# First scores in four banks, idle matmuls ahead of the loads, and other places for loads and conversions: an attention and mixing kernel on one core

## The chip, the core and the metric

The kernel runs on one core of a Trainium2 chip. The metric is the device time of one execution in microseconds; the median of three runs before the change is 418.61 us. The engines named are TensorE (PE; its weight loads stand as PEld), VectorE (DVE), ScalarE (ACT), GpSimd (POOL) and SyncE (SP), which here only issues loads and stores. ScalarE issues some of the first loads too.

## What is computed

Three blocks follow one another: local attention with a few global keys, a mixing block with a phase, and a gated feed-forward block. Cut to what matters:

```python
# attention: B=2, H=8, S=768, D=64; n_global=8, n_local=96
scores = scale * q @ k.T + bias(head, distance)       # masked to the local band and the global keys
a = exp(scores - max); a = a / (sum(a) + 1e-9)
x = a @ v                                             # heads side by side: [B, 768, 512]
# mixing
theta = x @ w_theta
y = w_tok_r @ (x * cos(theta)) + w_tok_i @ (x * sin(theta))   # along the tokens
u = x + y
x2 = u + relu(u @ w_ch)
# feed-forward
h = relu(x2 @ w_in)
c = depthwise_conv3(h, conv_w)
out = (h * sigmoid(c)) @ w_out
```

The weights w_theta, w_tok, w_ch, w_in, conv_w and w_out come as 64-bit floats.

## The kernel before

**Start.** `begin` (L942) loads the two words n_global and n_local and, for heads 0 and 1, q and k: three loads on SyncE's queue and three on ScalarE's (L950 to L953). A pair of heads shares one tile `qk`: the k of both stands in its two partition halves, the q of each beside zeros (`pad_q`), so that a score matmul runs over all 128 partitions. VectorE works out from the two words a flag `fi`, which says whether the fast path fits, and the mask table `Dt`. `build` then loads the flag on every engine and branches (L933, L936). `run_fast` (L799) is the fast path; the general path is not run here.

**Attention.** A step j is two query tiles of 128 rows of one head; there are 3 steps to a head and 48 steps (`NJ`). A step's parts are staggered over the loop of L834: at turn j TensorE makes the scores of step j into a bank S (two banks in turn), VectorE the softmax of step j-1 (L321, it reads the bank and writes `sS`, three buffers in turn), ScalarE the exponentials of j-2 (L330), TensorE the transposes of j-3 (L339), ScalarE their copy of j-4, TensorE the product with v of j-5 into a bank O (two in turn, one for a head), and VectorE the normalisation of a head (L274 to L276). In turns 0 to 7 VectorE also scales a mask table per head (L292). A head needs its v (`load_v`, L258, three buffers) and every second head the q and k of the next pair (`load_qk`, L224 and L225, two tiles). `load_qk_second` (L230) brings head 1's q. Each engine works through its own list in the order in which the code records it; nothing is reordered. SyncE's list of loads is one queue of this kind, too: a load that waits for a buffer holds all loads behind it.

**Theta and the conversions beside the attention.** After every sixth step the heads of 128 columns are transposed (`transpose_x`, L437, into a bank X), copied to `xT`, and split into two parts for two-part products (`split_xT`). From about step 34 on, theta of batch 0 is worked out, six matmuls a step, in the bank TH. A weight passes through six pieces: load, a (ScalarE, L117), b (VectorE, L122 and L123), c (VectorE, L129 and L130), d (ScalarE's rounding, L101) and e (VectorE's remainder, L109). `Net.weight` puts them on a list, and `net.run(k)` at the end of a turn records the next k of them. Four weights of w_theta and the first eight of w_tok, 72 pieces, are worked off in the attention's loop; the load of weight k+1 is recorded with the piece load of weight k. The number of pieces per turn is set by the last line of the loop:

```python
net.run(1 if j == 3 else 0 if j < 9 else 2)
```

**End of the attention.** When the last head is normalised, the last 128 columns are transposed in two halves, each into the only bank X (L860 to L863), with VectorE copying in between. Four theta products of batch 1 are opened meanwhile (`theta1_open`). Then `tail` follows (L620): the token products, w_ch, the feed-forward block.

Of the kernel before, what the change touches and what calls it, by code (L numbers as in the profile page):

```python
# [12 lines left out]
F32 = mybir.dt.float32  # L13
# [3 lines left out]
ALU = mybir.AluOpType  # L17
AX = mybir.AxisListType

B, H, S, D = 2, 8, 768, 64  # L20
DM, DFF = H * D, 1024
P = 128
NT = S // P
KC = DM // P
NF = DFF // P
NH = B * H
NG = 8
NPREV = P - NG
# [192 lines left out]
def load_qk(nc, io, t, i):  # L221


    nc.sync.dma_start(t[0:D, S:QK], io["qk"][i // 2, 0])  # L224
    nc.sync.dma_start(t[D:P, 0 : S + KK], io["qk"][i // 2, 1])  # L225


def load_qk_second(nc, io, t):

    nc.sync.dma_start(t[D:P, 0:S], io["qk"][0, 1][:, 0:S])  # L230


def pad_q(nc, t):
    nc.gpsimd.memset(t[D:P, S + KK : QK], 0.0)
    nc.gpsimd.memset(t[0:D, 0:S], 0.0)
# [45 lines left out]
class FastAttention(Attention):  # L281
# [15 lines left out]
    def scores(self, j):  # L297
        i, tp = divmod(j, 3)
        net = self.net
        Q, K = self.Q(i), self.K(i)  # L300
        sp = net.bank("S", 2)
        for u in range(2):
            t = 2 * tp + u
            if t == 0:
                o, r = sp[:, P : 2 * P], K[:, 0:P]
            else:
                o, r = sp[:, 256 * u : 256 * u + 256], K[:, KW * (t - 1) + NG : KW * t + P]
            net.mm(o, Q[:, t * P : t * P + P], r, True, True)
        self.state[j] = {"sp": sp}
# [98 lines left out]
class Mix:  # L408
# [6 lines left out]
    def begin(self):  # L415
        n = self.net
        self.xT = [n.slot(f"xT{b}", [P, KC, S], F32, "xT") for b in range(2)]
        wth = n.slot("w", [P, 2, KC, DM], F32R, "wth")
        self.wth = [wth[:, i] for i in range(2)]
        self.r = n.slot("r", [P, NT, DM], F32, "r")  # L420
        n.plan()
        for c in range(KC):
            n.weight(DM, self.wth[0][:, c], self.wth[1][:, c])
        self.wt = [[n.slot("p0", [P, 4, 2, HALF], F32R, "wt"), n.slot("p1", [P, 4, 2, HALF], F32R, "wt"), None], [None] * 3]
# [2 lines left out]
        n = self.net  # L427
        self.xTs = [n.slot(f"y{i}", [P, KC, S], F32R, "xTs") for i in range(2)]

    def transpose_x(self, b, c, e="A"):  # L430

        n = self.net
        for hf in range(2):
            xb = n.bank("X")
            for jj in range(3):
                t = 3 * hf + jj
                self.nc.tensor.transpose(xb[:, P * jj : P * jj + P], self.xs[b][:, t, P * c : P * c + P], n.head["ident"])  # L437
            yield
            n.hi(e, self.xT[b][:, c, HALF * hf : HALF * hf + HALF], xb[:, 0:HALF])
# [359 lines left out]
def run_fast(tc, net):  # L799
    nc, io = net.nc, net.io  # L800
    xs = [net.slot(f"xs{b}", [P, NT, DM], F32, "xs") for b in range(2)]
    att = FastAttention(net, xs)
    mix = Mix(net, xs)
    att.load_v(0)
    load_qk_second(nc, io, att.qk[0])
    att.load_v(1)
    load_qk(nc, io, att.qk[1], 2)
    mix.begin()
    mix.load_tok(0, 0)
    mix.load_tok(0, 1)  # L810
    net.drain()
    mix.alloc_xTs()
    NJ = 3 * NH
    OPEN = [NJ + 4, NJ + 6, NJ + 7, NJ + 8]
    first, last, splits, theta0 = Pipe(), Pipe(), deque(), None

    def theta_0():
        for t in range(NT):
            tiles = mix.theta(t, "TH", 1)
            for k in range(2):  # L820
                for _ in range(6):
                    th = next(tiles)
                yield
            first.add(mix.reduce_theta(th, mix.r[:, t]))

    early = mix.trig0()

    def split(b, c):
        yield
        yield  # L830
        yield
        splits.append((b, c))

    for j in range(NJ + LAG_N + 3):  # L834
        i, tp = divmod(j, 3)
        if j < NJ:
            att.scores(j)
        first.step()
        if 0 <= j - LAG_SM < NJ:
            att.softmax(j - LAG_SM)  # L840
        if tp == 0 and i < H:
            att.table(i)
        if 0 <= j - LAG_EXP < NJ:
            att.exps(j - LAG_EXP)
        if 0 <= j - LAG_T < NJ:
            att.transposes(j - LAG_T)
        if 0 <= j - LAG_EV < NJ:
            att.evacuate(j - LAG_EV)
        if 0 <= j - LAG_PV < NJ:
            att.pv(j - LAG_PV)  # L850
        jj = j - LAG_N
        if 0 <= jj < NJ and jj % 3 == 2:
            att.normalise(jj // 3, att.o.pop(jj // 3))
        if tp == 2 and i % 2 and i + 3 < NH:
            load_qk(nc, io, att.qk[i // 2 % 2], i + 3)
        if 0 < i < NH - 1 and tp == 2:
            att.load_v(i + 1)
        last.step()
        jj = j - LAG_N - 1
        if jj == NJ - 1:  # L860
            for chain in (mix.transpose_x(1, KC - 1, "V"), mix.split_xT(1, KC - 1, "V")):
                for _ in chain:
                    pass  # L863
        elif 0 <= jj < NJ and jj % 6 == 5:
            bc = divmod(jj // 6, KC)
            last.add(mix.transpose_x(*bc), split(*bc))
        if splits and (splits[0][0] == 0 or theta0 == "done"):
            b, c = splits.popleft()
            last.add(mix.split_xT(b, c, "V"))
            if (b, c) == (0, KC - 1):  # L870
                theta0 = theta_0()
        elif theta0 and theta0 != "done" and next(theta0, last) is last:
            theta0 = "done"
            mix.alloc_xTs()
        if j in OPEN:
            mix.theta1_open(OPEN.index(j))
        if j >= NJ + 4:
            next(early, None)
        net.run(1 if j == 3 else 0 if j < 9 else 2)
    last.drain()  # L880
    mix.tail(early)

# [37 lines left out]
def arm(tc, io, head, run):  # L920
    with tc.tile_pool(name="small", bufs=1) as small, tc.tile_pool(name="slots", bufs=1) as slots, tc.tile_pool(
        name="ps", bufs=1, space=bass.MemoryType.PSUM
    ) as ps, tc.manual_schedule():
        run(tc, Net(tc, io, small, slots, ps, head))


def build(nc, io):
    with tile.TileContext(nc) as tc, tc.tile_pool(name="const", bufs=1) as small:
        head = {}
        net = Net(tc, io, small, None, None, head)  # L930
        with tc.manual_schedule():
            begin(nc, io, net, small, head)
        rv = nc.values_load(  # L933
            head["flag"][:1, :1], min_val=0, max_val=1, skip_runtime_bounds_check_because="it is the product of comparisons, 0 or 1"
        )
        with tc.If(rv == 1) as cmp:  # L936
            arm(tc, io, head, run_fast)
        with cmp.Else():
            arm(tc, io, head, run_general)


def begin(nc, io, net, small, head):  # L942

    w = small.tile([P, 4], I32, name="words")
    scratch = small.tile([P, 2560], F32, name="scratch")
    nc.sync.dma_start(w, io["n"].bitcast(I32).rearrange("(o n) -> o n", o=1).to_broadcast([P, 4]))
    qk0 = small.tile([P, QK], F32, name="qk0")
    two, one = io["qk"][0, 0], io["qk"][0, 1]
    ks, qs = (slice(0, 2 * KW), slice(2 * KW, KK)), (slice(KK, KK + 2 * P), slice(KK + 2 * P, KK + S))
    for e, k, q in ((nc.sync, ks[0], qs[0]), (nc.scalar, ks[1], qs[1])):  # L950
        e.dma_start(qk0[0:D, S + k.start : S + k.stop], two[:, k])
        e.dma_start(qk0[D:P, S + k.start : S + k.stop], one[:, S + k.start : S + k.stop])
        e.dma_start(qk0[0:D, S + q.start : S + q.stop], two[:, q])  # L953
    pad_q(nc, qk0)
    cwb = small.tile([P, 2 * NF * 3], I32, name="cwb")

# [18 lines left out]
    ng, nl = f[:, 6:7], f[:, 7:8]  # L975
    flag = small.tile([1, 2], F32, name="flag")
    fi = small.tile([1, 1], I32, name="fi")
    nnl = small.tile([P, 1], F32, name="nnl")
    nc.vector.tensor_scalar(flag[:, 0:1], nl[0:1], 1.0, None, op0=ALU.is_ge)
    nc.vector.tensor_scalar(Dt[:, 0 : 2 * P], R[:, 0 : 2 * P], nl, BIG, op0=ALU.is_ge, op1=ALU.mult)  # L980
    nc.vector.scalar_tensor_tensor(flag[:, 1:2], nl[0:1], float(NPREV + 1), flag[:, 0:1], op0=ALU.is_le, op1=ALU.mult)
    nc.vector.tensor_scalar(Dt[:, NPREV:P], R[:, NPREV:P], ng, BIG, op0=ALU.is_ge, op1=ALU.mult)
    nc.vector.scalar_tensor_tensor(fi, ng[0:1], float(NG), flag[:, 1:2], op0=ALU.is_le, op1=ALU.mult)
    nc.vector.tensor_tensor(Dt[:, 0:NPREV], Dt[:, 0:NPREV], R[:, 0:NPREV], op=ALU.max)
    nc.vector.tensor_tensor(Dt[:, P : 2 * P], Dt[:, P : 2 * P], R[:, P : 2 * P], op=ALU.max)
    nc.vector.tensor_scalar(Dt[:, NPREV:P], Dt[:, NPREV:P], nl, None, op0=ALU.max)
# [39 lines left out]
```

## Time and profile before

| what | value |
|---|---|
| median of three runs | 418.61 us (418.59 to 419.8) |
| the profiled execution: its time | 418.75 us |
| its span, first instruction to last | 416.5 us |
| TensorE busy | 403.7 us, 97% |
| VectorE busy | 318.4 us, 76% |
| ScalarE busy | 236.8 us, 57% |
| first score matmul starts | 6.12 us |

The span is what the trace shows; 2.2 us of the execution's time lie around it. All times in the trace count from the span's start. A busy engine is one with an instruction under way. A matmul's end is modelled and overlaps with the next one's start, so that the distance from start to start tells more than a duration. A wait is put down to the semaphore that came last. In the row of granted clocks, as in the busy rows, a 9 is nine tenths or more. A product of 32-bit floats shows as two matmuls in the trace and as one in the order of instructions.

### The profile page before, as it was taken

Reading aid. Unit: us, or ns where it says so; the run is one execution under the profiler, and the core shown is the slowest. Engines: PE = TensorE matmul, PEld = TensorE weight load, DVE = VectorE, ACT = ScalarE, POOL = GpSimd, SP = SyncE. Lnnn points to the kernel's source line nnn. Section 1 sums busy time; section 2 is a strip of 40 time slices with the busy share of each in tenths; the row PEclk is TensorE's granted clock in tenths of the full one; section 3 lists DMA queues with packets and bytes.
Section 4 is the critical chain, followed back from the end, with each engine's and each line's share of the span. In section 5 each row is a group of like instructions: output and inputs, shape, how many; then the busy total and the mean of one; then the engine's idle time right before and its main releaser. Section 6 shows DMA issues by size and latency. Waiting matters only on the chain.

```text
span 416.5 us, 6402 instructions
## 1 busy us (share of the span) xinstructions
PE 403.7 (97%) x2376; PEld 379.2 (91%) x2376; DVE 318.4 (76%) x733; ACT 236.8 (57%) x449; POOL 4.4 (1%) x14
## 2 busy tenths in 40 slices
PE   4899999999999999999999999999999999999995
PEld 3899999988897899999999999999999998888885
DVE  4579999667568997899999999999699999800001
ACT  2777888685669536864436245446776889300000
POOL 4000000000000000000000000000000000000000
PEclk9999999999999999999999999999999999999999
DMA  6965776441420004006564352221000000111111
GB/s 168 255 177 178 214 226 161 123 131 35 142 84 2 0 9 144 2 1 188 178 202 155 101 169 84 63 91 52 0 2 0 2 0 0 53 49 50 52 50 58
DMA packets 13095, 38.03 MB, mean 91 GB/s; under 512 B 1856, under 2 KB 2304, under 8 KB 13056
## 3 DMA queue, kind: packets, MB, share of 16 engines
q1 hardware_dynamic: 12816, 37.13, 29.3%
q10 hardware_dynamic: 240, 0.41, 0.4%
q8 instruction: 20, 0.33, 0.3%
q14 instruction: 19, 0.16, 0.1%
HBM read 34.39 MB, written 3.15 MB: 90 GB/s over the span
## 4 chain that ended last, share of the span: by engine, by line
PE 95%; DMA 3%; DVE 1%; SPq 0%; issue 0%; DVEq 0%
PE O L112 26%; PE S L112 26%; PE PT L112 16%; PE TH L112 13%; PE X L112 9%; PE PT L339 4%; DMA qk<-qk 2%; PE X L437 1%; DMA words<-n 1%; SPq L258 0%; DVE a L321 0%; DVE xT L105 0%; SPq L224 0%; SPq L230 0%; DVE scratch L105 0%
## 5 line engine op out<-in xcount | busy, mean ns | idle before, releaser
L112 PE MATMUL S<-qk 128*128 128x256 f32 (+1 forms) x192 | 48.7, 380 | 7.4 <-DMA qk<-qk 7.2
L330 ACT ACTIVATE a<-a,nm 128x256 f32<-128x256 f32 (+1 forms) x96 | 41.5, 482 | 10.4 <-DVE nm L321 10.4
L321 DVE CUSTOM_DVE_ANT_0 a<-S,a 128x256 f32<-128x256 f32 (+1 forms) x96 | 34.5, 399 | 14.4 <-PE PT L339 12.3
L112 PEld LDWEIGHTS S<-qk 128*128 128x128 f32 x192 | 32.6, 198 | 11.1 <-issue 7.6
L101 ACT ACTIVATE a<-PT 128x512 f32<-128x512 f32 (+1 forms) x48 | 26.6, 554 | 11.2 <-PE PT L339 10.8
L112 PE MATMUL O<-a,a 128*128 128x65 f32 x236 | 29.8, 268 | 0.0
L112 PEld LDWEIGHTS O<-a,a 128*128 128x128 f32 x236 | 28.8, 192 | 0.0
L112 PE MATMUL PT<-wt,z 128*128 128x384 f32 x144 | 28.1, 335 | 0.0
L339 PE MATMUL PT<-ident,a 128*128 128x128 f32 x176 | 27.1, 273 | 0.0
L112 PE MATMUL O<-wt,z 128*128 128x384 f32 x144 | 26.9, 334 | 0.0
L339 PEld LDWEIGHTS PT<-ident,a 128*128 128x128 f32 x176 | 22.2, 141 | 4.5
L112 PE MATMUL S<-wt,z 128*128 128x384 f32 x144 | 26.2, 335 | 0.0
L101 ACT ACTIVATE wt<-wbit 128x384 fp32r<-128x384 f32 x24 | 12.5, 521 | 23.9 <-DVE wbit L130 23.9
L112 PE MATMUL TH<-wth,xTs 128*128 128x512 f32 x96 | 25.9, 406 | 0.0
L112 PEld LDWEIGHTS PT<-wt,z 128*128 128x128 f32 x144 | 25.3, 188 | 0.0
L112 PEld LDWEIGHTS O<-wt,z 128*128 128x128 f32 x144 | 25.2, 188 | 0.1
L112 PEld LDWEIGHTS S<-wt,z 128*128 128x128 f32 x144 | 25.2, 188 | 0.0
L117 ACT ACTIVATE wbit<-wst 128x384 f32<-128x384 f32 (+1 forms) x33 | 20.2, 612 | 3.3 <-DVE wout L109 1.1
L130 DVE SCALAR_TENSOR_TENSOR wbit<-wst,wbit 128x384 int32<-128x384 int32 (+1 forms) x33 | 20.6, 623 | 1.1
L129 DVE SCALAR_TENSOR_TENSOR wbit<-wst,wbit 128x384 int32<-128x384 int32 (+1 forms) x33 | 20.5, 622 | 0.9
L123 DVE TENSOR_SCALAR wbit<-wbit 128x512 int32<-128x512 int32 (+1 forms) x48 | 18.9, 394 | 1.6
L112 PEld LDWEIGHTS TH<-wth,xTs 128*128 128x128 f32 x96 | 17.1, 189 | 3.2
(180 smaller groups left out, 872.6 us busy)
## 6 DMA issues: line engine op xcount, KB each, us to landing
wst<-w_tok SPq DMA_DIRECT2D x17, 384.0 KB, 4.6
a<-v SPq DMA_DIRECT2D x16, 357.5 KB, 4.8
qk<-qk SPq DMA_DIRECT2D x14, 396.0 KB, 5.7
out<-scratch SPq DMA_DIRECT2D x11, 256.0 KB, 2.0
qk<-w_tok SPq DMA_DIRECT2D x7, 384.0 KB, 3.3
wst<-w_out SPq DMA_DIRECT2D x5, 512.0 KB, 3.4
wst<-w_theta SPq DMA_DIRECT2D x4, 512.0 KB, 7.6
qk<-w_in SPq DMA_DIRECT2D x4, 512.0 KB, 3.4
```

Of the source, the lines that this page charges most:

```text
L101: self.nc.scalar.activation(out, in_, AF.Copy)
L112: self.nc.tensor.matmul(out, l, r, start=start, stop=stop)
L117: self.nc.scalar.activation(t.bitcast(F32), w[:, 1 : w.shape[1] : 2].bitcast(F32), AF.Abs)
L123: nc.vector.tensor_scalar(t, t, 3, 0x3FFFFFFF, op0=ALU.logical_shift_left, op1=ALU.bitwise_and)
L129: nc.vector.scalar_tensor_tensor(t, lo, 29, t, op0=ALU.logical_shift_right, op1=ALU.bitwise_or)
L130: nc.vector.scalar_tensor_tensor(t, hi, -(1 << 30), t, op0=ALU.bitwise_and, op1=ALU.bitwise_or)
L321: nc.vector.tensor_tensor_reduce(sS[:, c], s["sp"][:, c], self.T[i % H][:, 256:TW] if t0 else self.T[i % H][:, 0:256], scale=-0.125, scala ...
L330: self.nc.scalar.activation(sS[:, rng[u]], sS[:, rng[u]], AF.Exp, bias=nm[:, u : u + 1], scale=-1.0)
L339: self.nc.tensor.transpose(pt[:, c], sS[:, c], net.head["ident"])
L437: self.nc.tensor.transpose(xb[:, P * jj : P * jj + P], self.xs[b][:, t, P * c : P * c + P], n.head["ident"])
```

## The change

It has five parts.

1. `warm` sets 128 columns of scratch to zero on VectorE and puts eleven 128x128 products of them on TensorE, ahead of the flag's load, into a bank of a pool that ends with `begin`.
2. The first loads of q and k: both parts of q go on ScalarE's queue and ahead of its k; SyncE's queue carries the words and its part of k. The flag is computed ahead of the mask table.
3. Steps 0 to 3 have their scores recorded in turns 0 and 1, into the banks S, S, X and TH; turns 2 and 3 record none.
4. The load of q and k of heads 2 and 3 is recorded ahead of v of head 1. The numbers of pieces per turn become 1 in turn 5, 1 and 2 in turns 10 to 31, 2 and 3 from turn 32 on.
5. The second half of the last transposes goes into a bank O.

The diff, cut (the banks' argument is also passed through `transpose_x`, and the two flag instructions move up by two lines):

```diff
-        sp = net.bank("S", 2)
+        sp = net.bank("X") if j == 2 else net.bank("TH") if j == 3 else net.bank("S", 2)
...
-            xb = n.bank("X")
+            xb = n.bank(*second) if hf else n.bank("X")
...
     load_qk_second(nc, io, att.qk[0])
+    load_qk(nc, io, att.qk[1], 2)
     att.load_v(1)
-    load_qk(nc, io, att.qk[1], 2)
...
-        if j < NJ:
-            att.scores(j)
+        for x in ((0, 1), (2, 3), (), ())[j] if j < 4 else (j,) if j < NJ else ():
+            att.scores(x)
...
-            for chain in (mix.transpose_x(1, KC - 1, "V"), mix.split_xT(1, KC - 1, "V")):
+            for chain in (mix.transpose_x(1, KC - 1, "V", ("O", 2)), mix.split_xT(1, KC - 1, "V")):
...
-        net.run(1 if j == 3 else 0 if j < 9 else 2)
+        net.run(1 if j == 5 else 0 if j < 10 else 1 + j % 2 if j < 32 else 2 + j % 2)
...
+def warm(nc, z, idle):
+    nc.vector.memset(z, 0.0)
+    o = idle.tile([P, 512], F32, name="idle")
+    for _ in range(11):
+        nc.tensor.matmul(o[:, 0:P], z, z, start=True, stop=True)
...
+    warm(nc, scratch[:, 2432:2560], idle)
...
-    for e, k, q in ((nc.sync, ks[0], qs[0]), (nc.scalar, ks[1], qs[1])):
+    for x, (k, q) in enumerate(zip(ks, qs)):
+        nc.scalar.dma_start(qk0[0:D, S + q.start : S + q.stop], two[:, q])
+        e = nc.scalar if x else nc.sync
         e.dma_start(qk0[0:D, S + k.start : S + k.stop], two[:, k])
         e.dma_start(qk0[D:P, S + k.start : S + k.stop], one[:, S + k.start : S + k.stop])
-        e.dma_start(qk0[0:D, S + q.start : S + q.stop], two[:, q])
```

SyncE's queue right behind the branch, before the change. The tiles a_3, a_4 and a_5 hold v, qk_63 the tile of heads 0 and 1, qk_6 that of heads 2 and 3, wst the raw weights:

```order
L936 COMPARE_AND_BRANCH
L258 DMA a_3_130<-v 128x715
L230 DMA qk_63<-qk 64x768
L258 DMA a_4_131<-v 128x715
L224 DMA qk_6_133<-qk 64x1584
L225 DMA qk_6_133<-qk 64x1584
L144 DMA wst_145<-w_theta 128x1024
L144 DMA wst_146<-w_theta 128x1024
L224 DMA qk_63<-qk 64x1584
```

The same place after the change (qk_79 is the tile of heads 0 and 1):

```order
L936 COMPARE_AND_BRANCH
L258 DMA a_3_147<-v 128x715
L230 DMA qk_79<-qk 64x768
L224 DMA qk_6_150<-qk 64x1584
L225 DMA qk_6_150<-qk 64x1584
L258 DMA a_4_148<-v 128x715
L224 DMA qk_79<-qk 64x1584
L225 DMA qk_79<-qk 64x1584
L258 DMA a_5_149<-v 128x715
L144 DMA wst_162<-w_theta 128x1024
L144 DMA wst_163<-w_theta 128x1024
```

The second v and the two loads of heads 2 and 3 have changed places, and the first two weights stand behind the loads of heads 4 and 5 and the third v.

TensorE at the start, before the change; S, PT and O are banks, the first product from qk_6 is head 2's:

```order
L933 TENSOR_LOAD fi
L936 COMPARE_AND_BRANCH
L112 MATMUL S_152<-qk_63 128x128
L112 MATMUL S_152<-qk_63 128x256
L112 MATMUL S_156<-qk_63 128x256 x2
L112 MATMUL S_162<-qk_63 128x256 x2
L112 MATMUL S_170<-qk_63 128x128
L112 MATMUL S_170<-qk_63 128x256
L339 MATMUL PT_179<-ident,a_5_132 128x128 x3
L112 MATMUL S_185<-qk_63 128x256 x2
```

The same after the change:

```order
L947 MATMUL idle<-scratch 128x128 x11
L933 TENSOR_LOAD fi
L936 COMPARE_AND_BRANCH
L112 MATMUL S_169<-qk_79 128x128
L112 MATMUL S_169<-qk_79 128x256
L112 MATMUL S_172<-qk_79 128x256 x2
L112 MATMUL X_176<-qk_79 128x256 x2
L112 MATMUL TH_179<-qk_79 128x128
L112 MATMUL TH_179<-qk_79 128x256
L339 MATMUL PT_196<-ident,a_5_149 128x128 x3
L112 MATMUL S_200<-qk_79 128x256 x2
```

TensorE's list is the same but for the idle products and the banks of the third and fourth step.

VectorE around the second weight's pieces b (L122, L123) and c (L129, L130), before the change; the lines L321 are a softmax:

```order
L321 ISA a_5_132,nm_378<-S_350,a_4_131 128x256
L321 ISA nm_378 128x1
L122 TENSOR_SCALAR wbit_318<-wbit_318 128x512
L123 TENSOR_SCALAR wbit_318<-wbit_318 128x512
L129 SCALAR_TENSOR_TENSOR wbit_318<-wst_146,wbit_318 128x512
L130 SCALAR_TENSOR_TENSOR wbit_318<-wst_146,wbit_318 128x512
L321 ISA a_5_132,nm_405<-S_375,a_4_131 128x256
```

After the change, for the same weight:

```order
L122 TENSOR_SCALAR wbit_360<-wbit_360 128x512
L123 TENSOR_SCALAR wbit_360<-wbit_360 128x512
L321 ISA a_5_149,nm_463<-S_437,a_4_148 128x128
L321 ISA nm_463 128x1
L321 ISA a_5_149,nm_463<-S_437,a_4_148 128x256
L321 ISA nm_463 128x1
L109 TENSOR_TENSOR xTs_168<-xT_158,xTs_167 128x768
L129 SCALAR_TENSOR_TENSOR wbit_360<-wst_163,wbit_360 128x512
```

The four passes stood in one row between two softmaxes; now a softmax stands between b and c.

## Rows read from the trace of the kernel before

**Rows 1.** The page: busy tenths and granted clock in 40 slices of 10.4 us

```profile
PE   4899999999999999999999999999999999999995
...
DVE  4579999667568997899999999999699999800001
...
PEclk9999999999999999999999999999999999999999
```

**Rows 2.** Waits of TensorE, whole run: us in total, times, longest us

```profile
PE S L112 <- DMA qk<-qk: 7.2, 2, 6.1
PE X L437 <- DVE xT L105: 0.7, 1, 0.7
```

**Rows 3.** Timeline, 0 to 16 us: start us, us, engine line op, count [idle before <-releaser]

```profile
4.25 0.33 DVE L980 TENSOR_SCALAR Dt<-scratch,nf 128x256 f32<-128x256 f32 x1
...
4.75 0.14 DVE L983 SCALAR_TENSOR_TENSOR fi<-nf,flag 1x1 int32<-1x1 f32 x1
...
5.54 0.35 SPq L258 DMA_DIRECT2D a<-v  x1
...
5.93 0.47 SPq L230 DMA_DIRECT2D qk<-qk  x1
...
7.58 0.59 SPq L225 DMA_DIRECT2D qk<-qk  x1
...
10.33 0.52 PEld L112 LDWEIGHTS S<-qk 128*128 128x128 f32 x4 [0.33 <-issue]
...
14.02 0.78 PE L112 MATMUL O<-a 128*128 128x65 f32 x6
...
15.91 0.89 PE L112 MATMUL S<-qk 128*128 128x128 f32 x4 [1.10 <-DMA qk<-qk]
```

**Rows 4.** Loads L230, v of head 1, L225, first w_theta: KB each, us to landing

```profile
qk<-qk SPq DMA_DIRECT2D x1, 192.0 KB, 3.9
...
a<-v SPq DMA_DIRECT2D x1, 357.5 KB, 5.6
...
qk<-qk SPq DMA_DIRECT2D x1, 396.0 KB, 8.2
...
wst<-w_theta SPq DMA_DIRECT2D x1, 512.0 KB, 8.9
```

**Rows 5.** TensorE by form, 6 to 9.2 and 11.4 to 14 us: xcount | busy, mean ns

```profile
L112 PE MATMUL S<-qk 128*128 128x256 f32 x6 | 2.8, 634 | 0.0
...
L112 PE MATMUL S<-qk 128*128 128x256 f32 x8 | 2.1, 380 | 0.0
```

**Rows 6.** Timeline of VectorE and of TensorE, 52 to 54 us

```profile
52.34 0.56 DVE L130 SCALAR_TENSOR_TENSOR wbit<-wst,wbit 128x384 int32<-128x384 int32 x1
...
52.71 0.78 PE L112 MATMUL O<-a 128*128 128x65 f32 x6
53.64 0.92 PE L112 MATMUL S<-qk 128*128 128x128 f32 x4
```

**Rows 7.** Timeline of TensorE, 129 to 131 us: the last transposes

```profile
129.17 0.49 PE L437 MATMUL X<-ident,xs 128*128 128x128 f32 x3
130.31 0.55 PE L437 MATMUL X<-ident,xs 128*128 128x128 f32 x3 [0.65 <-DVE xT L105]
130.62 0.72 PE L112 MATMUL S<-wth,xTs 128*128 128x512 f32 x2
```

**Rows 8.** Timeline of ScalarE and of TensorE, 22 to 29 us

```profile
22.11 0.68 ACT L117 ACTIVATE wbit<-wst 128x512 f32<-128x512 f32 x1
...
24.44 0.79 ACT L330 ACTIVATE a<-a,nm 128x128 f32<-128x128 f32 x2
...
27.40 0.78 PE L112 MATMUL O<-a,a 128*128 128x65 f32 x6
28.02 0.87 PE L112 MATMUL S<-qk 128*128 128x128 f32 x4
28.73 0.49 PE L339 MATMUL PT<-ident,a 128*128 128x128 f32 x3
```

More of the change, by code (lines that the diff above doesn't have):

```diff
@@ L428, in alloc_xTs, with transpose_x @@
         self.xTs = [n.slot(f"y{i}", [P, KC, S], F32R, "xTs") for i in range(2)]
-    def transpose_x(self, b, c, e="A"):
+    def transpose_x(self, b, c, e="A", second=("X", 1)):
         n = self.net
         for hf in range(2):
-            xb = n.bank("X")
+            xb = n.bank(*second) if hf else n.bank("X")
             for jj in range(3):
@@ L930, in build @@
         net = Net(tc, io, small, None, None, head)
-        with tc.manual_schedule():
-            begin(nc, io, net, small, head)
+        with tc.tile_pool(name="idle", bufs=1, space=bass.MemoryType.PSUM) as idle, tc.manual_schedule():
+            begin(nc, io, net, small, head, idle)
         rv = nc.values_load(
@@ L939, in build, with begin @@
             arm(tc, io, head, run_general)
-def begin(nc, io, net, small, head):
+def warm(nc, z, idle):
[3 more added lines that the diff above has]
+        nc.tensor.matmul(o[:, 0:P], z, z, start=True, stop=True)
+def begin(nc, io, net, small, head, idle):
     w = small.tile([P, 4], I32, name="words")
     scratch = small.tile([P, 2560], F32, name="scratch")
+    warm(nc, scratch[:, 2432:2560], idle)
     nc.sync.dma_start(w, io["n"].bitcast(I32).rearrange("(o n) -> o n", o=1).to_broadcast([P, 4]))
@@ L979, in begin @@
     nc.vector.tensor_scalar(flag[:, 0:1], nl[0:1], 1.0, None, op0=ALU.is_ge)
+    nc.vector.scalar_tensor_tensor(flag[:, 1:2], nl[0:1], float(NPREV + 1), flag[:, 0:1], op0=ALU.is_le, op1=ALU.mult)
+    nc.vector.scalar_tensor_tensor(fi, ng[0:1], float(NG), flag[:, 1:2], op0=ALU.is_le, op1=ALU.mult)
     nc.vector.tensor_scalar(Dt[:, 0 : 2 * P], R[:, 0 : 2 * P], nl, BIG, op0=ALU.is_ge, op1=ALU.mult)
-    nc.vector.scalar_tensor_tensor(flag[:, 1:2], nl[0:1], float(NPREV + 1), flag[:, 0:1], op0=ALU.is_le, op1=ALU.mult)
     nc.vector.tensor_scalar(Dt[:, NPREV:P], R[:, NPREV:P], ng, BIG, op0=ALU.is_ge, op1=ALU.mult)
-    nc.vector.scalar_tensor_tensor(fi, ng[0:1], float(NG), flag[:, 1:2], op0=ALU.is_le, op1=ALU.mult)
     nc.vector.tensor_tensor(Dt[:, 0:NPREV], Dt[:, 0:NPREV], R[:, 0:NPREV], op=ALU.max)
```

## The prediction

> **What bounds the kernel now.** I read the busy slices first: TensorE is at nine tenths in all 40 slices but the first two and the last [rows 1]. So I asked only where TensorE stands still. The table of waits has two lines for it: 7.2 us behind loads of q and k, in two places, and 0.7 us behind a VectorE copy [rows 2]. The timeline places them. The first wait ends at 6.1 us with the first scores [rows 2]. The second comes after the fourth step's work: the first P·V product starts at 14.02, the next score matmul only at 15.91, released by a load of q and k [rows 3]. In steady work the next scores start 0.62 us after such a product starts (27.40 to 28.02 [rows 8]), so TensorE could have gone on at 14.64: 1.27 us are lost there. The chain of the attention also has a stop that the waits don't list: at 52.71 a product of the same shape starts and the scores follow at 53.64, 0.93 later instead of 0.62 [rows 6]; VectorE had put two conversion passes ahead of the softmax that frees the score bank (the last of them starts at 52.34). 0.3 us, and some 0.1 us for a refill of the pipeline, are lost. At 129.17 the last transposes start; three of them hold the engine for some 0.3 us (130.31 to 130.62, where the next matmul starts), so the second three could start at 129.5 and start at 130.31 [rows 7]: 0.8 us. Everything else is TensorE's own work, which the change leaves alone but for the idle matmuls. **So the most the change can take out of the middle is 1.27 + 0.4 + 0.8 us; the rest must come from the start.**
>
> **The start: when do scores 0 to 3 begin and end?** Scores 3 are head 1's first; they need the late load of head 1's q (L230), which is issued after the branch. Before, it was issued at 5.93 and took 3.9 us: landed at 9.83. Scores 3 began at 10.33, just behind scores 2 [rows 3, 4]. They had been slow until then: a 256-column pass took 634 ns up to 9.2 us and 380 ns later [rows 5], so TensorE ran at the lower of its two levels (1.2 GHz) at first and at 2.4 GHz afterwards, though the row of granted clocks has nines, nine tenths or more, from the first slice on [rows 1].
>
> Step by step after the change. (1) Before, the flag was written at 4.75 and the first load behind the branch issued at 5.54. In the half microsecond between 4.25, where the first mask instruction starts, and 4.75 stand three instructions of VectorE [rows 3]; now one of them stands ahead of the flag, which I put 0.2 us earlier, and with it L258 and L230, at about 5.34 and 5.73. (2) L230 still stands second behind the branch; with the same 3.9 us it lands at 9.63. (3) Scores 0 to 2 no longer wait for a free score bank, and with the idle matmuls they may run at the upper level. The q of scores 0 goes first on ScalarE's queue instead of last on SyncE's. I expect scores 0 at about 5.6 and scores 2 done by 8 us at the upper level, by about 10 at the lower one. **At the upper level none of that moves the end, since scores 3, next in TensorE's order, wait for L230 anyway.** So the idle matmuls and the extra two banks are worth nothing beyond bringing TensorE to that wait; I take 9.7 for scores 3 instead of 10.33, a gain of 0.6. If the load is as quick as its neighbour or quicker, up to 0.6 more; if it is slowed by the two large loads now right behind it, the gain is nothing.
>
> (4) From scores 3 to the next head's scores the order of TensorE is what it was: 10.33 to 14.64, 4.3 us, all work. ScalarE and VectorE have what it needs: the first exponentials follow softmax 0, and TensorE comes no faster than before from there. So TensorE asks for heads 2 and 3 at 9.7 + 4.3 = 14.0. (5) Their load: before, v of head 1, L224 and L225 were issued in this order behind L230, and L225 landed at 7.58 + 8.2 = 15.8, so three loads of 357.5 + 396 + 396 KB came in the 5.95 us after 9.83: 193 KB/us [rows 3, 4]. Now v stands behind the two: 792 KB after 9.63 at that rate are 4.1 us, so L225 lands at 13.7, ahead of 14.0. **The 1.27 us of waiting go, and with the 0.6 the attention's main stretch begins at 14.0 instead of 15.91: 1.9 us.** The margin is only 0.3, so a part of a microsecond may come back. A rule of the Trainium skill bears on this order: DMA: Bandwidth & Descriptors, "Queues, rings and completion order", says that an engine works through one ring in order and that completions need not follow the order of issue. By the first half the reorder is worth all of v's share; by the second L225 could still land with v, and that would be the first rival below. The rows stand nearer to the first: L230, issued 1.65 us ahead of L225, landed 6 us ahead of it [rows 3, 4].
>
> **What moves later.** The two first loads of w_theta stood ahead of the loads of heads 4 and 5 and now stand behind them and behind v of head 2. They are issued at about 14.8 us. At 193 KB/us, behind v of head 1 (landing 15.5), q and k of heads 4 and 5 (792 KB) and v (358 KB), the first lands at about 24. It was wanted at 22.11 [rows 8] in step 9 and is now wanted one step later, about 22.3 on the moved clock. So ScalarE can stand still some 2 us. Who waits for that: the exponentials and copies queued behind it. They run far ahead: the exponentials of step 9 start at 24.44, are over 0.8 us later, and are used by transposes at 28.73 [rows 8], 3.5 us of slack. One step's two exponentials (0.79 us the pair [rows 8]) and one copy are about 1.5 us of a step of some 2.1, so it catches up. I cost this at nothing; without that cover it is 2 us. The third weight, issued behind the loads of heads 6 and 7, has about the same slack. Bounds: 0 to 1.5 us.
>
> **The spread conversions.** Before, two pieces a step from step 9 on; VectorE stands at nine tenths in the slices from 31 to 73 us and at five to seven tenths in those from 73 to 125 [rows 1]. The change gives 1.5 a step up to step 31 and 2.5 from there, where VectorE has room, and puts the two halves of a conversion on either side of a softmax. The number of pieces is the same (72, used up at step 47 instead of 44), and the weights are done before the theta and token products ask for them (the last piece of w_theta at step 29, theta from step 34). TensorE's gain is only the stop at 53 us: 0.4. Bounds: 0 to 0.4 while nothing new stops.
>
> **The last transposes.** The second three go to the bank O, free since head 14 was normalised, so they need not wait for the copy: 0.8 us. The copy and split are needed some 7 us later.
>
> **Sum**, against the profiled execution's own 418.75 us (span 416.5 and 2.2 around it): 0.6 + 1.27 + 0.4 + 0.8 = 3.1, so 415.65. The median of the three runs is 418.61, 0.14 lower, so 415.5 against it; I say 415.6.
>
> **Rivals.** *The loads still set the pace* (12 in 100). L225 lands at 15.6 because the engines share the packets of all loads in flight, or L230 is late. For it: they were busy without a gap there. Then only 0.3 + 0.4 + 0.8 us go: 417.2; if the stop at 53 us stays too, 417.6. *The clock is low at scores 3* (7 in 100). TensorE stands still between scores 2 and 3, for up to 1.7 us; if the lower level holds or comes back there for as long as it held before (6.1 to at least 9.2 [rows 2, 5]), half of that stretch is lost, 1.6: 417.2. The 1.1 us of idling at 14.8 didn't bring it back, which speaks against. The Trainium skill, TensorE: Matmul & The Clock Gate, Part 1, says that the point at which the clock rises varies from run to run of one kernel, by which the idle matmuls may not be in time; no run here shows such a variation yet. *The weights come so late that ScalarE stops TensorE* (5 in 100, the slow side). ScalarE works in order, so a missing w_theta holds exponentials and copies for TensorE. Its price is the lateness beyond the 3.5 us of slack; the gain of 3.1 is eaten when a weight comes 6.6 us after it is wanted, that is at 29 us or later for the first, and it is slower than before by over 0.3% from 30.2 on: 420. The longest way of a weight before was 8.9 us for the first [rows 4]; it would have to be over 14. *The idle matmuls hold the branch* costs nothing: eleven cold ones are over by about 6, and scores 3 wait longer.
>
> **How the numbers follow.** Forecast 415.6 with 76 in 100, the rivals as above. A measurement can tell about 0.3% from no change, 1.26 us. Faster by more than that: the forecast, and most of the second and half of the first rival, 0.85. Within it: the rest of these, 0.10. Slower: 0.05. Range: downward, 0.6 for a quicker L230 and 0.3 for a median under the profile, 414.7; upward past both fast rivals, 417.4.
>
> **What would show it.** In the profile after: L230 lands 9.4 to 9.9 and the fourth scores start right there; the wait for q and k ahead of head 2's scores is gone or under 0.5 us, and these start near 14.0; no stop of TensorE near 50; the last six transposes in one row; the waits for weights on ScalarE new, 1 to 3 us, without one on TensorE. Wrong if scores 3 start before 9 (then the idle matmuls paid), if head 2's scores start after 15, or if TensorE shows a new wait between 20 and 40.

## The result

The median of four runs is 415.41 us (415.2 to 416.23); the kernel before, run beside it, took 418.73 us (418.59 to 419.8, four runs). The ratio is 0.9918, with a 95% interval of 0.9905 to 0.9932: 3.3 us faster, where 3.1 against the profiled execution and a time of 415.6 were forecast. The profiled execution is the slowest of the four (416.23, span 414.1), so two more profiles of the same kernel stand among the experiments.

The waits of TensorE after the change (columns as in [rows 2]):

```profile
PE TH L112 <- DMA qk<-qk: 1.8, 1, 1.8
PE idle L947 <- DVE hp L974: 1.1, 1, 1.1
PE S L112 <- PE idle L947: 0.2, 1, 0.2
```

Of the two waits for q and k, 7.2 us together [rows 2], the one ahead of the first scores has given way to the idle products, and the one ahead of head 2's scores is gone. A new one stands ahead of scores 3 (bank TH); before, TensorE came there just behind scores 2. The copy that held the last transposes is gone as well. The timeline after (columns as in [rows 3]; the flag, SyncE's loads, TensorE at the start, and TensorE at the last transposes):

```profile
1.05 4.72 PE L947 MATMUL idle<-scratch 128*128 128x128 f32 x22 [1.05 <-DVE hp L974]
...
4.48 0.15 DVE L991 SCALAR_TENSOR_TENSOR fi<-nf,flag 1x1 int32<-1x1 f32 x1
...
5.66 0.47 SPq L230 DMA_DIRECT2D qk<-qk  x1
5.99 1.76 PE L112 MATMUL S<-qk 128*128 128x128 f32 x8 [0.21 <-PE idle L947]
...
6.80 0.59 SPq L225 DMA_DIRECT2D qk<-qk  x1
7.58 1.03 PE L112 MATMUL X<-qk 128*128 128x256 f32 x4
10.42 0.89 PE L112 MATMUL TH<-qk 128*128 128x128 f32 x4 [1.81 <-DMA qk<-qk]
...
14.08 0.78 PE L112 MATMUL O<-a 128*128 128x65 f32 x6
14.70 0.87 PE L112 MATMUL S<-qk 128*128 128x128 f32 x4
...
127.56 0.49 PE L437 MATMUL X<-ident,xs 128*128 128x128 f32 x3
127.89 0.49 PE L437 MATMUL O<-ident,xs 128*128 128x128 f32 x3
128.13 3.05 PE L112 MATMUL S<-wth,xTs 128*128 128x512 f32 x12
```

The reader is to see four places. The flag is 0.27 us earlier and L230 is issued at 5.66 instead of 5.93 [rows 3]. Scores 2 end by 8.6, and then TensorE stands until 10.42. From the first P·V product (14.08) to head 2's scores it is 0.62 us, the distance of steady work [rows 8], where it was 1.89 [rows 3]. The last six transposes stand in a row. The landings of L230 and L225 (columns as in [rows 4]):

```profile
qk<-qk SPq DMA_DIRECT2D x1, 192.0 KB, 4.6
...
qk<-qk SPq DMA_DIRECT2D x1, 396.0 KB, 7.5
```

L230 lands at 5.66 + 4.6 = 10.26, later than before (9.83), and scores 3 start right behind it; L225 lands at 6.80 + 7.5 = 14.3, ahead of 14.70. The score passes of 256 columns from 6 to 9 us (columns as in [rows 5]):

```profile
L112 PE MATMUL S<-qk 128*128 128x256 f32 x6 | 1.5, 380 | 0.0
```

They take 380 ns where they took 634 [rows 5]: TensorE is at the upper level, 2.4 GHz, from the first scores on. The busy slices (as in [rows 1], 10.35 us each):

```profile
PE   7999999999999999999999999999999999999995
...
DVE  5568988775779997999999999999699999800000
```

VectorE's stretch from 31 to 73 us, nine tenths before [rows 1], now reads eight and nine tenths: pieces have moved behind it.

**The account of this execution**, by TensorE's starts: head 2's scores 15.91 to 14.70, 1.21 us; from there to the last transposes another 0.40 (129.17 to 127.56 is 1.61); from these to the next matmul another 0.88 (130.62 to 128.13 is 2.49). That is 2.49 in all; the spans differ by 2.4 (416.5 to 414.1). The start gave nothing here, since L230 was late; in the other two profiles of the same kernel it gave 0.85 and 0.92 (scores 3 at 9.51 and 9.44, from 10.36 before).

### The profile page after: what moved, and what is told of

Read it like the earlier page. It is cut to its first block, busy times and chain, and to the rows that moved or that the text cites. A ratio compares the mean times of both kernels' runs of the same rounds, so it can differ in the third digit from the quotient of the medians.

```text
span 414.1 us, 6441 instructions
## 1 busy us (share of the span) xinstructions
PE 406.1 (98%) x2398; PEld 382.2 (92%) x2398; DVE 317.8 (77%) x734; ACT 236.9 (57%) x449; POOL 4.4 (1%) x14
## 3 DMA queue, kind: packets, MB, share of 16 engines
HBM read 34.39 MB, written 3.15 MB: 91 GB/s over the span
## 4 chain that ended last, share of the span: by engine, by line
PE 96%; DMA 2%; DVE 0%; SPq 0%; issue 0%; DVEq 0%
PE O L112 26%; PE S L112 26%; PE PT L112 16%; PE TH L112 13%; PE X L112 9%; PE PT L339 5%; PE X L437 1%; DMA qk<-qk 1%; DMA words<-n 1%; DVE scratch L105 0%; SPq L258 0%; PE O L437 0%; DVE Dt L992 0%; SPq L933 0%; DVE nf L982 0%
## 5 line engine op out<-in xcount | busy, mean ns | idle before, releaser
L112 PE MATMUL S<-qk 128*128 128x256 f32 (+1 forms) x184 | 45.2, 369 | 0.2 <-PE idle L947 0.2
L321 DVE CUSTOM_DVE_ANT_0 a<-S,a 128x256 f32<-128x256 f32 (+1 forms) x92 | 33.1, 399 | 12.2 <-PE PT L339 8.1
L112 PEld LDWEIGHTS S<-qk 128*128 128x128 f32 x184 | 30.0, 191 | 3.1 <-issue 0.4
L130 DVE SCALAR_TENSOR_TENSOR wbit<-wst,wbit 128x384 int32<-128x384 int32 (+1 forms) x33 | 20.6, 623 | 1.1
L129 DVE SCALAR_TENSOR_TENSOR wbit<-wst,wbit 128x384 int32<-128x384 int32 (+1 forms) x33 | 20.5, 621 | 0.7
L123 DVE TENSOR_SCALAR wbit<-wbit 128x512 int32<-128x512 int32 (+1 forms) x48 | 18.9, 394 | 1.6
## 6 DMA issues: line engine op xcount, KB each, us to landing
a<-v SPq DMA_DIRECT2D x16, 357.5 KB, 5.4
```

The costliest lines, as they stand in the source:

```text
L112: self.nc.tensor.matmul(out, l, r, start=start, stop=stop)
L123: nc.vector.tensor_scalar(t, t, 3, 0x3FFFFFFF, op0=ALU.logical_shift_left, op1=ALU.bitwise_and)
L129: nc.vector.scalar_tensor_tensor(t, lo, 29, t, op0=ALU.logical_shift_right, op1=ALU.bitwise_or)
L130: nc.vector.scalar_tensor_tensor(t, hi, -(1 << 30), t, op0=ALU.bitwise_and, op1=ALU.bitwise_or)
L321: nc.vector.tensor_tensor_reduce(sS[:, c], s["sp"][:, c], self.T[i % H][:, 256:TW] if t0 else self.T[i % H][:, 0:256], scale=-0.125, scala ...
```

## Experiments

Each is the changed kernel with one edit, unless said otherwise; each was timed beside the kernel before. The theory, A: L230's landing paces scores 3, L225's head 2's scores, and the rest of the attention follows by the same amount. The rival, B: what counts is when TensorE reaches the upper level, and the loads are hidden.

**The changed kernel, unchanged (a_again, a_third).**

> The changed kernel as it is, beside the same runs of before. Theory A (loads pace the start): 415.2 to 415.6; where L230 (head 1's q) lands at 9.6 to 9.9, scores 3 start right behind it and the execution is some 0.5 us under the one profiled (416.23, L230 landed at 10.26). Theory B (the spread comes from the clock's rise during the idle matmuls): the time does not follow L230's landing, but the point at which the passes become short.

> The changed kernel once more, as the measure for the two beside it: 415.2 to 415.6, scores 3 right behind L230's landing near 9.4.

415.32 us (0.9909, 0.9884 to 0.9934) and 415.61 us (0.9902, 0.9881 to 0.9922). In a_again L230 landed at 5.68 + 3.7 = 9.38. Its timeline and L230's issue row:

```profile
1.05 5.06 PE L947 MATMUL idle<-scratch 128*128 128x128 f32 x22 [1.05 <-DVE hp L974]
...
9.51 0.89 PE L112 MATMUL TH<-qk 128*128 128x128 f32 x4 [0.29 <-DMA qk<-qk]
...
13.79 0.87 PE L112 MATMUL S<-qk 128*128 128x128 f32 x4
```

```profile
qk<-qk SPq DMA_DIRECT2D x1, 192.0 KB, 3.7
```

The same 22 idle passes lasted longer than in the first profile (5.06 against 4.72), so TensorE rose later, and yet scores 3 came 0.91 earlier, with the earlier landing. Span 413.1 against 414.1. For A. In a_third L230 landed at 9.3 and scores 3 started at 9.44; L225 landed at 13.7:

```profile
13.10 0.78 PE L112 MATMUL O<-a 128*128 128x65 f32 x6
...
13.88 0.89 PE L112 MATMUL S<-qk 128*128 128x128 f32 x4
```

From the first P·V product to head 2's scores it is 0.78 us here, 0.16 more than in steady work: L225 came a little too late. So there are two gates, what holds scores 3 and what holds head 2's scores, and in the changed kernel they open almost in step: no margin is left at the second.

**Without the idle products (b_no_idle).**

```diff
-    for _ in range(11):
+    for _ in range(0):
```

> The changed kernel without the eleven idle products. Theory A (scores 3 wait for L230 whatever came before): scores 0 to 2 run at the lower level and end near 9.8; scores 3 start at 10.0 to 10.4; the time is 0 to 0.4 us above the changed kernel. Theory B (the idle matmuls carry the gain at the start): scores 3 start at 10.4 or later and the work behind it too, 1 us or more above the changed kernel.

416.6 us (415.57 to 416.98), 1.3 over a_again in the same rounds; spans 414.0 and 413.1. Timeline of b_no_idle, and its passes from 5.6 to 9 us:

```profile
5.63 3.33 PE L112 MATMUL S<-qk 128*128 128x128 f32 x8 [5.63 <-DVE Dt L995]
8.74 1.69 PE L112 MATMUL X<-qk 128*128 128x256 f32 x4
10.27 0.82 PE L112 MATMUL TH<-qk 128*128 128x128 f32 x4
...
14.48 0.87 PE L112 MATMUL S<-qk 128*128 128x128 f32 x4
```

```profile
L112 PE MATMUL S<-qk 128*128 128x256 f32 x6 | 2.8, 634 | 0.0
```

L230 had landed at 9.7, but the row of scores 3 names no load: TensorE was still at scores 0 to 2, at 634 ns a pass, until 10.27. So A's price (0 to 0.4) was wrong, and the time is the one that B named (1 us or more). The idle products give 0.76 of the 0.85 us at the start (10.27 against 9.51, from 10.36 before). The gate at scores 3 is the later of L230 and the slow scores, and without idle products the slow scores are the later. The profile shows 0.9 of the medians' 1.3 us (its execution, 416.21, is the second fastest of seven); where the others lose the rest stays open.

**The idle products alone, on the kernel before (j_idle_only).** The kernel before, with `warm` and its pool and nothing else.

> The kernel before with the eleven idle products alone. Theory A: scores 0 to 2 become short, scores 3 start at L230's landing, 9.8 to 9.9 instead of 10.36, but L225 still lands near 15.8 and head 2's scores with it: within 0.3 us of before. Rival (the idle products carry about 1 us by themselves): 0.8 us or more below before.

420.02 us (418.4 to 422.27) against 419.32: ratio 1.001, 0.999 to 1.0031, no gain, as A had it. Six of its twelve executions took over 420 us, and three of the seventeen of the kernel before; the profiled one (421.78) is one of the six. Its timeline, the landing of L225, and three stretches of it (from:to, us, busy time of PE, PEld, DVE, ACT and POOL, granted clock, DMA share, GB/s):

```profile
9.66 0.89 PE L112 MATMUL S<-qk 128*128 128x128 f32 x4 [0.31 <-DMA qk<-qk]
...
13.32 0.78 PE L112 MATMUL O<-a 128*128 128x65 f32 x6
17.25 1.24 PE L112 MATMUL S<-qk 128*128 128x128 f32 x4 [3.15 <-DMA qk<-qk]
```

```profile
qk<-qk SPq DMA_DIRECT2D x1, 396.0 KB, 9.6
```

```profile
14.00:17.60 3.60, 0.45 (x4) 0.38 (x4) 0.46 (x3) 0.91 (x3) 0.00 (x0) 1.00 1.00 251
17.70:21.00 3.30, 3.30 (x15) 2.99 (x14) 0.73 (x4) 1.18 (x3) 0.00 (x0) 0.50 1.06 207
21.10:24.00 2.90, 2.90 (x21) 2.62 (x20) 1.51 (x7) 1.39 (x3) 0.00 (x0) 1.00 0.79 165
```

Scores 3 start 0.7 earlier than before, and all of it is waited away ahead of head 2's scores, since L225 still stands behind v of head 1. Here it also landed late (7.55 + 9.6 = 17.15), and after that stand the granted clock was 0.50, the lower level, for 3.3 us: some 1.7 us more. With the 1.34 by which head 2's scores are later than before (17.25 and 15.91), that is the 3.0 us between 421.78 and the profile of before (418.75). This is the clock rival of the prediction, seen in a combination that the change avoids. In this kernel the idle products pay only together with the order of the loads. Whether the other five long executions have the same cause is not shown.

**The loads in their old order (c_v_first).** `load_v(1)` ahead of `load_qk` again.

> The changed kernel with v of head 1 ahead of the loads of heads 2 and 3 again. Theory A (loads land in the order of issue): L225 lands some 1.5 to 2 us later, near 16, TensorE waits 1.2 to 1.8 us ahead of head 2's scores, and the time is 1.2 to 1.8 us above the changed kernel. Rival (the engines share the packets of all loads in flight, so the order means little; the weights that no longer compete made the room): L225 lands within 0.5 us of where it does in the changed kernel, and the time is within 0.5 us.

416.99 us, 1.7 over a_again. Timeline and L225's issue row of c_v_first:

```profile
13.62 0.78 PE L112 MATMUL O<-a 128*128 128x65 f32 x6
15.34 0.89 PE L112 MATMUL S<-qk 128*128 128x128 f32 x4 [0.94 <-DMA qk<-qk]
```

```profile
qk<-qk SPq DMA_DIRECT2D x1, 396.0 KB, 7.4
```

L225 is issued at 7.78 and lands at 15.2, and 1.1 us of the wait are back (15.34 − 13.62 − 0.62). The other 0.45 of the 1.55 by which head 2's scores are late against a_again is a later start of this execution (scores 3 at 9.96). The loads land in the order of issue, and v's place in the list is worth most of v's bytes: apart from the later start, L225 lands 1.3 us later than in a_again, where 357.5 KB take 1.85 us at the 193 KB/us of the prediction. In the changed kernel v lands only 0.5 to 0.9 us behind L225, so part of its bytes travelled beside L225's. The Trainium skill, DMA: Bandwidth & Descriptors, "Queues, rings and completion order", has both that a ring is worked through in order and that a later transfer may complete first; these runs agree with the first, and none shows the second.

**The old number of pieces per turn (d_old_runs).**

```diff
-        net.run(1 if j == 5 else 0 if j < 10 else 1 + j % 2 if j < 32 else 2 + j % 2)
+        net.run(1 if j == 3 else 0 if j < 9 else 2)
```

> The changed kernel with the old number of conversion pieces per turn (one in turn 3, two from turn 9 on). Theory A: the stop of 0.3 to 0.4 us near 50 us comes back and nothing else, 0.4 us above the changed kernel. Rival (the first two weights, issued in turn 3 again right behind v of head 1, take room from the loads ahead of them): L225 lands later than 15 and the time is 1 us or more above the changed kernel.

415.92 us, 0.6 over a_again; spans 413.7 and 413.1. Timeline of d_old_runs at the stop:

```profile
50.27 0.56 DVE L130 SCALAR_TENSOR_TENSOR wbit<-wst,wbit 128x384 int32<-128x384 int32 x1
...
50.64 0.78 PE L112 MATMUL O<-a 128*128 128x65 f32 x6
...
51.57 0.92 PE L112 MATMUL S<-qk 128*128 128x128 f32 x4 [0.15 <-DVE nm L321]
```

From product to scores it is 0.93 us again, as in [rows 6], and 0.62 in a_again (50.57 to 51.19); by the last transposes 0.47 is lost, 0.05 of it from the start. Of the 0.42 that is left, 0.31 is lost between product and scores and another 0.08 by the second product behind them (51.57 to 55.16, against 51.19 to 54.70 in a_again). The forecast 0.4 holds. The rival is out: the first two weights are issued at 8.09 again, and head 2's scores start at 13.84 all the same.

**Both halves of the last transposes in bank X (e_x_bank).**

```diff
-mix.transpose_x(1, KC - 1, "V", ("O", 2))
+mix.transpose_x(1, KC - 1, "V")
```

> The changed kernel with both halves of the last transposes in the bank X again. Theory A: the wait for VectorE's copy, 0.8 us between the two halves, comes back and is the whole difference: 0.8 us above the changed kernel (415.3). Rival (VectorE's split behind it sets the theta products' last part, so the wait is hidden elsewhere): under 0.3 us.

416.82 us, 1.3 over f_two_banks in the same rounds; spans 414.2 and 413.2. Timeline of e_x_bank:

```profile
126.67 0.49 PE L437 MATMUL X<-ident,xs 128*128 128x128 f32 x3
127.81 0.55 PE L437 MATMUL X<-ident,xs 128*128 128x128 f32 x3 [0.65 <-DVE xT L105]
128.11 1.65 PE L112 MATMUL S<-wth,xTs 128*128 128x512 f32 x6
```

The wait of [rows 7] is back: the next matmul starts at 128.11 against 127.22 in a_again, from an almost equal start of the transposes (126.67 and 126.65): 0.87 more on the way. The spans differ by about that, the medians by 0.3 more, which the intervals allow (0.9928 to 0.9956, and 0.9898 to 0.9926).

**Two score banks, one step a turn (f_two_banks).** `net.bank("S", 2)` for all, `att.scores(j)` at turn j.

> The changed kernel with the scores of steps 0 to 3 in the two banks S in turn, recorded in turns 0 to 3 as before. Theory A: steps 2 and 3 wait for softmax 0 and 1 (read by 8.2 and 8.9 us), ahead of L230's landing near 9.4; scores 3 start where they do in the changed kernel and the time is within 0.3 us of it. Rival (four banks carry part of the gain): 0.5 us or more above.

415.55 us (0.9912, 0.9898 to 0.9926), within 0.3 of the changed kernel. TensorE waits for a bank, and then has scores 2 done in time for L230 (5.66 + 3.6 = 9.3) all the same. Timeline of f_two_banks; the first row holds scores 2 and 3:

```profile
8.29 1.99 PE L112 MATMUL S<-qk 128*128 128x256 f32 x8 [0.76 <-DVE nm L321]
...
13.71 0.89 PE L112 MATMUL S<-qk 128*128 128x128 f32 x4
```

The two extra banks are worth nothing here.

**Head 1's q ahead of the branch (g_q1_early), and that without idle products (g_no_idle).** If L230 is the gate, taking it out of the way shows the next one.

```diff
+    nc.sync.dma_start(qk0[D:P, 0:S], one[:, 0:S])
     pad_q(nc, qk0)
...
-    load_qk_second(nc, io, att.qk[0])
```

> The changed kernel with head 1's q (L230's 192 KB) loaded ahead of the branch, last on SyncE's first queue, instead of behind it. Theory A (L230 paces the start): scores 3 start right behind scores 2, near 8.5 with the early clock and 9.1 with the late one, and head 2's scores 0.4 to 1.0 us earlier than 13.8; L225 has less ahead of it, lands by 12.5, and the time is 0.4 to 1.0 us below the changed kernel. Rival (the exponentials or L225 pace the steps behind scores 3): within 0.3 us.

> As the one before, without the eleven idle products. Theory A: with the load out of the way the slow passes of scores 0 to 3 are the pace; they run at the lower level from 5.6 us for some 4.4 us, so scores 3 end near 10.8 instead of 9.2 and the time is 1.3 to 2.0 us above the kernel with the idle products. Rival (in the kernel without idle products the 1.3 us came from elsewhere): under 0.7 us.

415.1 us (0.9901, 0.9887 to 0.9915): only 0.2 to 0.5 under the changed kernel. Timeline of g_q1_early:

```profile
7.59 1.10 PE L112 MATMUL S<-qk 128*128 128x256 f32 x4 [0.92 <-DMA qk<-qk]
...
9.39 0.82 PE L112 MATMUL TH<-qk 128*128 128x128 f32 x4
```

The 192 KB now travel beside ScalarE's k, whose second part lands at 7.4 instead of 6.4, and scores 1 wait for it: A's gain of 0.4 to 1.0 was missed because the wait moved ahead by two steps. Without idle products the time is 416.94, 1.84 more than g, as A had it; scores 3 start at 10.97 and head 2's scores at 15.17 (13.59 in g). With the load gone from the gate, the slow passes cost 1.58 us at head 2's scores.

**L230 first behind the branch (i_l230_first).** `load_qk_second` ahead of `att.load_v(0)`.

> The changed kernel with L230 first behind the branch and v of head 0 second. Theory A (L230 paces scores 3, and the bytes ahead of L225 stay the same): L230 lands near 8.4, scores 3 start right behind scores 2 or L230 (8.4 to 9.2), head 2's scores near 12.9, set by L225's landing (12.8 in the changed kernel); 0.4 to 0.9 us below it. Rival (as with head 1's q ahead of the branch, the loads only trade places and the wait moves to v of head 0): within 0.3 us.

415.48 us, 0.1 under a_third in the same rounds: A's 0.4 to 0.9 was missed. Timeline of i_l230_first and the issue row of L225 (issued at 7.02):

```profile
8.49 0.89 PE L112 MATMUL TH<-qk 128*128 128x128 f32 x4
...
12.15 0.78 PE L112 MATMUL O<-a 128*128 128x65 f32 x6
13.72 0.89 PE L112 MATMUL S<-qk 128*128 128x128 f32 x4 [0.79 <-DMA qk<-qk]
```

```profile
qk<-qk SPq DMA_DIRECT2D x1, 396.0 KB, 6.6
```

Scores 3 do start 0.95 earlier than in a_third (9.44), and 0.95 is waited away ahead of head 2's scores (13.72 − 12.15 − 0.62): L225 lands at 13.6, where it lands at 13.4 in a_again and 13.7 in a_third. The 12.8 that the expectation gives for the changed kernel stands in no profile of it; with 13.4 to 13.7 the loss of the gain could have been forecast. Opening the first gate alone moves the wait to the second.

**Only the bytes that the next steps read (k_split).** L230 first, and of heads 2 and 3 first only what their first steps read (two blocks of k of both, two tiles of head 2's q: 68, 68 and 64 KB) on ScalarE's queue; the rest behind v of head 0, and head 3's q behind v of head 1:

```diff
-    att.load_v(0)
     load_qk_second(nc, io, att.qk[0])
-    load_qk(nc, io, att.qk[1], 2)
+    t1, two1, one1 = att.qk[1], io["qk"][1, 0], io["qk"][1, 1]
+    nc.scalar.dma_start(t1[0:D, S : S + 2 * KW], two1[:, 0 : 2 * KW])
+    nc.scalar.dma_start(t1[D:P, S : S + 2 * KW], one1[:, S : S + 2 * KW])
+    nc.scalar.dma_start(t1[0:D, S + KK : S + KK + 2 * P], two1[:, KK : KK + 2 * P])
+    att.load_v(0)
+    nc.sync.dma_start(t1[0:D, S + 2 * KW : S + KK], two1[:, 2 * KW : KK])
+    nc.sync.dma_start(t1[D:P, S + 2 * KW : S + KK], one1[:, S + 2 * KW : S + KK])
+    nc.sync.dma_start(t1[0:D, S + KK + 2 * P : QK], two1[:, KK + 2 * P : KK + S])
     att.load_v(1)
+    nc.sync.dma_start(t1[D:P, 0:S], one1[:, 0:S])
```

> A version meant to beat the changed kernel: L230 first behind the branch; of heads 2 and 3 the columns that head 2's first step reads (204 KB) go on ScalarE's queue at once, the rest on SyncE's behind v of head 0, head 3's q last. Theory A (what holds head 2's scores near 13.7 is the bytes that must land ahead of L225's end): the first columns land by 10, scores 3 start near 8.5 and head 2's scores near 12.7, no wait for loads ahead of them; 0.8 to 1.1 us below the changed kernel, 414.3 to 414.7. Rival (the wait only moves on, to v of head 0 or to head 2's second step): within 0.3 us of it, with a wait of 0.5 us or more at one of those two.

414.53 us (414.44 to 414.73), ratio 0.9895, 0.9879 to 0.9912: 0.8 to 1.1 under the changed kernel, and faster than both kernels. All four spans are 412.2 to 412.6; those of the three profiles of the changed kernel 413.1 to 414.1. Timeline and last wait of k_split:

```profile
8.63 0.89 PE L112 MATMUL TH<-qk 128*128 128x128 f32 x4 [0.23 <-DMA qk<-qk]
...
12.91 0.87 PE L112 MATMUL S<-qk 128*128 128x128 f32 x4
```

```profile
PE TH L112 <- DMA qk<-qk: 0.2, 1, 0.2
```

Both gates open 0.9 earlier than in a_again, and no wait is left behind the first one. The first columns of heads 2 and 3 land by 11.2 (10 was expected), ahead of the scores that need them. L230 in first place is worth 0.1 alone (i_l230_first); the other 0.9 comes from the fewer bytes, from ScalarE's queue, or from both, which no run tells apart.

## Why the prediction was right

**The order of the loads: right in mechanism and size.** L225 was to land at 13.7 and to be wanted at 14.0. It landed at 13.4 to 14.3 in the three profiles of the changed kernel, wanted at 13.7 to 14.7. The 1.27 us went in two of them, and 1.11 in a_third; c_v_first brought 1.1 back. The first rival (loads shared by all in flight) is out as what sets the pace, though v's landing close behind L225 shows some sharing; its other half, a late L230, is the first profile.

**The start: right in size, wrong in what gives it.** The term was 0.6, with L230 landing at 9.63. It landed at 9.38, 9.26 and 10.26 in a_again, a_third and the first profile, and the term measured 0.85, 0.92 and nothing, which follows the landing. The step that failed is the sentence that the idle matmuls are worth nothing beyond bringing TensorE to the wait. The working had the number in hand, scores 2 done "by about 10 at the lower one", and set it beside a landing of 9.63 without drawing the difference. Before the change, too, L230 had landed at 9.83 and scores 3 came half a microsecond later, at 10.36, behind the slow scores 2: an earlier landing alone could give nothing there. So the size was met in part by luck. b_no_idle gives 10.27 against 9.51: without idle products 0.76 of the 0.85 is lost, and 1.3 in the medians. The sign named for it, scores 3 before 9, was badly chosen too: they started at 9.4 to 10.4, and the idle products paid all the same. The extra banks were put right: f_two_banks. That the idle products hold the first scores at no cost was right as well: scores 0 start at 5.99 and 6.33 (first profile, a_again) and at 5.63 without them, and scores 2 are still done ahead of L230. The earlier flag and the new order of the first loads were not undone by themselves; the flag's 0.27 us is read from the profile.

**The stop at 53 us: right.** 0.40 against 0.4; d_old_runs loses 0.42.

**The last transposes: right.** 0.88 against 0.8; e_x_bank loses 0.87.

**The weights that come later: right.** The forecast was some 2 us of ScalarE's waiting without a stop of TensorE; the three profiles show 0.3 us (the first), 1.5 us in two waits (a_again) and 1.0 us (a_third) for w_theta, and TensorE's waits have no line for it.

**The clock rival.** TensorE stood 1.81 us ahead of scores 3 and the four passes behind it last 0.89 us, as they do in a_again behind a stand of 0.29: no fall there. j_idle_only shows the fall after a longer stand, 3.15 us.

**The sum.** 0.85 + 1.27 + 0.40 + 0.88 = 3.4 for a_again, whose span is 3.4 shorter than before (416.5 to 413.1); 3.1 was forecast; the difference is the start's 0.85 against 0.6 and the transposes' 0.88 against 0.8. In the first profile the start gave nothing, since L230 landed late. Why that load takes 4.6 us in the first profile and 3.6 to 4.0 in the others that have it in the same place stays open; no run was made on it.

## What to carry to other kernels

At a start, write down for each gate what closes it, the load and the engine's own work at either clock, and take the later: an edit on one side pays only down to the other, and an edit that is worth nothing alone (idle products on the kernel before, j) can be worth 1.3 us beside another (b). Then look for the next gate before pulling a load forward: twice the wait simply moved (g, i), and only the version that also brought the bytes of the second gate forward (k) moved the end by more than half a microsecond. A row of long vector passes is best kept off the operation that frees a bank: it cost 0.4 us here (d).

## What the runs showed of the hardware

The time at which TensorE rises to its upper level varies from run to run of the same start: the same 22 passes of idle products, begun at 1.05 or 1.06, took from 4.12 us (c_v_first, where a pass took 421 ns at first and 275 ns at the end) to 5.06 us (a_again, where none was that short). The Trainium skill, TensorE: Matmul & The Clock Gate, Part 1, says so; these rows agree. A stand of 1.81 us was not followed by the lower level, one of 3.15 us was, for the next 3.3 us at a granted clock of 0.50 (j_idle_only). And one load of 192 KB in the same place of the list landed 3.7 and 4.6 us after its issue in two executions of the same kernel, one of 396 KB after 8.2 us [rows 4] and 9.6 us in the same order of loads.
